# First k of block 0 loaded and turned by itself; block 1's first turns split around a gate product

## The chip, the cores and the metric

The kernel runs on one core of a Trainium2 chip. The metric is the device time of one execution in microseconds (us), the lower the better. A profile gives the same execution from inside: PE is the tensor engine (matrix products; PEld its weight loads), DVE the vector engine, ACT the scalar engine, POOL the engine that issues the converting loads, SP a further issuing engine. Every run also carries the mean clock that was granted to PE.

## The reference, cut to what matters

Linear attention with decay, then a gated feed-forward layer over all tokens:

```python
# q, k, v: (4 batches, 8 heads, 768 positions, 64); weights 512 x 1536, 512 x 1536, 1536 x 512
intra = einsum(q_block, k_block) * decay_mask ; intra = intra @ v_block
inter = (q_block * lam_pow) @ kv_state          # state carried from block to block
x = (intra + inter) as 3072 tokens x 512
out = (sigmoid(x @ w_gate) * (x @ w_val)) @ w_out
```

The kernel works on six blocks of 128 positions. Block 0 has no state yet. The feed-forward layer of a block is cut into 12 units of 128 hidden columns: a gate product, a sigmoid on ACT, a value product, and their product on DVE.

## The kernel before

The traces have each engine's instructions in the order of the program text (before, PE: turns of q 0 from 5.79 us, of q 1 from 6.68, of k 0 and 1 from 7.57, scores from 8.65; ACT: copies of k from 8.01). Only parts are shown. "Turning" is a transpose on PE by a product with the identity; the turned q is scaled by DVE, the turned k is copied out of PSUM by ACT.

```python
# loads, all issued by POOL on one software queue, in this order
load(0, "k", 0, 2)            # k of block 0, batches 0 and 1, one load
load(0, "k", 2, 4)
load(0, "q", 2, 3); load(0, "q", 3, 4)      # q of batches 0 and 1 come by other queues
load(0, "v", 0, 1); load(0, "v", 1, 2); load(0, "v", 2, 3)
load_w(WG, wg_r, 0, GW // 2); load_w(WV, wv_r, 0, GW // 2)   # unit 0
load(0, "v", 3, 4)
load_w(WG, wg_r, 1, GW // 2); load_w(WV, wv_r, 1, GW // 2)   # unit 1: loads 11 and 12
load_w(WG, wg_r, 2, GW // 2)                                 # unit 2, gate: load 13
# ... more weights

def idle(n):                  # dummy products of zeros
    for i in range(n):
        nc.tensor.matmul(wm, lhsT=zero[:, :C], rhs=zero, ...)     # 512 columns

# the start, PE's order
idle(10)
piece_tq0([0]); make_mask(0); idle(1); piece_tq0([1])
piece_tk0(0)                  # turns and copies of k, batches 0 and 1
make_mask(1); idle(1)
piece_s(0, [0]); piece_m(0, 0)              # scores (PE), mask product (DVE)
piece_s(0, [1]); piece_m(0, 1, (0,))
piece_tk0(1)                  # batches 2 and 3
nc.scalar.preload_act_table_set("sigmoid_and_others")
piece_tq0([2]); piece_tq0([3])
piece_m(0, 1, (1,))
piece_s(0, [2], ps_ff, "ff"); piece_m(0, 2); piece_s(0, [3]); piece_m(0, 3)
# ... products with v, casts of x on ACT (piece_a0), first gate product g0

# later, block 1 beside unit 9 of block 0
gv(0, 8)
t(1, 0)                       # turn q, scale; turn k, copy
gv(0, 9)                      # gate product, sigmoid, value product, product
sc(1, 0); m(1, 0)             # scores of block 1
```

Of the kernel before, what the change touches and what calls it, by code (L numbers as in the profile page):

```python
# [8 lines left out]
BF16 = mybir.dt.bfloat16  # L9
# [6 lines left out]
def kernel(  # L16
# [11 lines left out]
    nc = tc.nc  # L28

    B, H, S, D = q.shape  # L30
    C = 128
    NSTEP = S // C
    HP = H // 2
# [4 lines left out]
    TCH = B * C  # L38
# [5 lines left out]
    trsb = ctx.enter_context(tc.tile_pool(name="trsb", bufs=3))  # L44
# [6 lines left out]
    ps_at = ctx.enter_context(tc.tile_pool(name="ps_at", bufs=5, space=bass.MemoryType.PSUM))  # L51
# [9 lines left out]
    WG = const.tile([128, NMT, DFF], BF16, tag="WG")  # L61
    WV = const.tile([128, NMT, DFF], BF16, tag="WV")
# [5 lines left out]
    Q, K, V = {}, {}, {}  # L68

    def load(n, what, b0, b1):  # L70
        sl = slice(n * C, (n + 1) * C)
        for c in what:
            lst, src = {"q": (Q, q), "k": (K, k), "v": (V, v)}[c]
            if n > 1 and c != "v":
                lst[n] = qkv.tile([128, 2, B, HP, D], BF16, tag=c + "b", name=c + "b")
                for e in range(2):
                    nc.gpsimd.dma_start(  # L77
                        out=lst[n][:, e].rearrange("p b y d -> p (b y) d"),
                        in_=src[:, e::2, sl, :].rearrange("b y s d -> s (b y) d"))
                continue  # L80
            if n == 1 and c != "v":
                if n not in lst:
                    lst[n] = qkv.tile([128, 2, B * H * D // 2], BF16, tag=c + "b", name=c + "b")
                for e in range(2):
                    nc.gpsimd.dma_start(
                        out=lst[n][:, b0 // 2].rearrange("p (e x d) -> p e x d", e=2, d=D)[:, e],
                        in_=src[b0:b1, e::2, sl, :].rearrange("b y s d -> s (b y) d"))
                continue
            if n not in lst:
                lst[n] = qkv.tile([128, B, H, D], BF16, tag=c + "b", name=c + "b")  # L90
            nc.gpsimd.dma_start(  # L91
                out=lst[n][:, b0:b1],
                in_=src[b0:b1, :, sl, :].rearrange("b h s d -> s (b h) d"))
# [18 lines left out]
    ident = const.tile([128, 128], BF16, tag="ident")  # L112
# [19 lines left out]
    nc.vector.tensor_scalar(out=ident, in0=ip1, scalar1=p1, scalar2=None, op0=ALU.is_equal)  # L132
    nc.vector.tensor_scalar(out=tri, in0=ip1, scalar1=p1, scalar2=None, op0=ALU.is_ge)

    load(0, "k", 0, 2)
    load(0, "k", 2, 4)
    load(0, "q", 2, 3)
    load(0, "q", 3, 4)
# [61 lines left out]
    def masked(out, x, n, u):  # L200
        if n == 0:
            nc.vector.tensor_tensor(out=out, in0=x, in1=mask[:, u::2, :], op=ALU.mult)
            return
        nc.vector.tensor_tensor(  # L204
            out=out.rearrange("p (e x) c -> p e x c", e=2), in0=x.rearrange("p (e x) c -> p e x c", e=2),
            in1=mask.rearrange("p (x u e) c -> p u e x c", u=2, e=2)[:, u], op=ALU.mult)
# [7 lines left out]
    QS, KS, MT, XT, KD = {}, {}, {}, {}, {}  # L214

    QR, HB = {}, {}
# [20 lines left out]
    def transpose_pair(out, x, b, g):  # L237
        nc.tensor.transpose(out, x[:, b, 2 * g:2 * g + 2, :].rearrange("p h d -> p (h d)"), ident)  # L238

    def scale(n, bp, src):  # L240
        QS[n, bp] = trsb.tile([128, 2, 2, 2, C], BF16, tag="QS", name="QS")
        nc.vector.tensor_tensor(out=QS[n, bp].rearrange("p e i x c -> p e i (x c)"),
                                in0=src.rearrange("p e i x c -> p e i (x c)"),
                                in1=lamq_e.unsqueeze(2).to_broadcast([128, 2, 2, 2 * C]), op=ALU.mult)

    def piece_tq0(bs, then=None):
        tq = ps_at.tile([128, 2, 2, 2 * C], BF16, name="tq", tag="ps")
        for b in bs:
            if (0, b // 2) not in QS:
                QS[0, b // 2] = trsb.tile([128, 2, 2, 2, C], BF16, tag="QS", name="QS")  # L250
            for g in range(HP):
                transpose_pair(tq[:, b % 2, g // 2, g % 2 * C:g % 2 * C + C], Q[0], b, g)
        if then:
            then()
        for b in bs:
            nc.vector.tensor_tensor(out=QS[0, b // 2][:, :, b % 2].rearrange("p e x c -> p e (x c)"),
                                    in0=tq[:, b % 2], in1=lamq0_e, op=ALU.mult)

    def piece_tk0(bp):
        KS[0, bp] = trsb.tile([128, 2, 2, 2, C], BF16, tag="KS", name="KS")  # L260
        for i in range(2):
            if i == 0 or bp == 0:
                tk = ps_at.tile([128, 1 + bp, 2, 2 * C], BF16, name="tk", tag="ps")
            x = tk[:, i if bp else 0]
            for g in range(HP):
                transpose_pair(x[:, g // 2, g % 2 * C:g % 2 * C + C], K[0], 2 * bp + i, g)
            nc.scalar.copy(KS[0, bp][:, :, i].rearrange("p e x c -> p e (x c)"), x)  # L267

    def piece_t(n, bp):
        if n > 1 or bp == 1:  # L270
            scale(n, bp, QR[n][:, :, 2 * bp:2 * bp + 2] if n > 1 else HB["q"])
            return
        q1, k1 = (x[1][:, 0].rearrange("p (e b y d) -> p e b y d", e=2, b=2, y=HP) for x in (Q, K))
        tq = ps_at.tile([128, 2, 2, 2, C], BF16, name="tq", tag="ps")
        tk = ps_at.tile([128, 2, 2, 2, C], BF16, name="tk", tag="ps")

        def turn(out, x):
            for e in range(2):
                for i in range(2):
                    for g in range(2):  # L280
                        nc.tensor.transpose(out[:, e, i, g, :],
                                            x[:, e, i, 2 * g:2 * g + 2, :].rearrange("p y d -> p (y d)"), ident)

        turn(tq, q1)
        scale(n, bp, tq)
        turn(tk, k1)
        KS[n, bp] = trsb.tile([128, 2, 2, 2, C], BF16, tag="KS", name="KS")
        nc.scalar.copy(KS[n, bp], tk)

    SP = {}  # L290

    def piece_s(n, bs, pool=ps_at, tag="ps"):

        for b in bs:
            bp, i = b // 2, b % 2
            sp = [pool.tile([128, HP, C], FP32, name=f"sp{u}", tag=tag) for u in range(2)]
            for hp in range(HP):
                for u in range(2):
                    us = slice(u * 64, (u + 1) * 64)
                    nc.tensor.matmul(sp[u][:, hp, :], lhsT=KS[n, bp][us, hp // 2, i, hp % 2, :],  # L300
                                     rhs=QS[n, bp][us, hp // 2, i, hp % 2, :],
                                     start=(hp == 0), stop=(hp == HP - 1), skip_group_check=True)
            SP[n, b] = sp

    def piece_m(n, b, us=(0, 1)):
        if us[0] == 0:
            MT[n, b] = mtp.tile([128, 2, HP, C], BF16, tag="MT", name="MT")
        for u in us:
            masked(MT[n, b][:, u], SP[n, b][u], n, u)
# [121 lines left out]
    def mm_part(ps, W, n, ft, lo, hi):  # L431
        x = XT[n].rearrange("p m b c -> p m (b c)")
        for mt in range(NMT):
            nc.tensor.matmul(ps[:, lo:hi], lhsT=W[:, mt, ft * 128:(ft + 1) * 128], rhs=x[:, mt, lo:hi],  # L434
                             start=(mt == 0), stop=(mt == NMT - 1))

    def psum():
        return ps_ff.tile([128, TCH], FP32, name="gp", tag="ff")

    def sigm(n, ft, gp):  # L440
        HT[n, ft] = htp.tile([128, TCH], BF16, tag="sg", name="sg", bufs=3)
        nc.scalar.activation(HT[n, ft], gp, AF.Sigmoid)

    def prod(n, ft, vp):
        sg = HT[n, ft]
        HT[n, ft] = htp.tile([128, TCH], BF16, tag="ht", name="ht", bufs=2 * NFT)
        nc.vector.tensor_mul(HT[n, ft], sg, vp)
# [55 lines left out]
    idle(1)  # L503
    piece_tq0([1])
    piece_tk0(0)
    make_mask(1)
    idle(1)
    piece_s(0, [0])
    piece_m(0, 0)
    piece_s(0, [1])  # L510
    piece_m(0, 1, (0,))
    piece_tk0(1)
    nc.scalar.preload_act_table_set("sigmoid_and_others")
    piece_tq0([2])
    piece_tq0([3])
    piece_m(0, 1, (1,))
    piece_s(0, [2], ps_ff, "ff")
    piece_m(0, 2)
    piece_s(0, [3])
# [26 lines left out]
    def t(n, bp):  # L546
        piece_t(n, bp)

    def sc(n, bp):
        piece_s(n, [2 * bp, 2 * bp + 1])  # L550
        piece_m(n, 2 * bp)
# [7 lines left out]
    def gv(n, *fts):  # L559
        for ft in fts:  # L560
            piece_gv(n, ft)
# [36 lines left out]
    lamq_end()  # L598
    gv(0, 6, 7)
    gv(0, 8)  # L600
    t(1, 0)
    gv(0, 9)
    sc(1, 0)
    m(1, 0)
    gv(0, 10)
# [101 lines left out]
```

## Time and profile before

226.63 us, median of three runs (226.24 to 227.24). The profiled run had a span of 224.5 us at full clock.

| reading | value |
|---|---|
| PE busy | 97% of the span |
| chain of waits on PE | 94% |
| first gate product of unit 0 starts | 14.51 us |
| gate, value product of unit 1 start | 17.16, 18.03 us |
| turn of block 1's q, its scores start | 31.45, 34.34 us |

The first part of the page (busy time, share and instructions of each engine):

```profile
PE 217.8 (97%) x1746; PEld 114.7 (51%) x1746; DVE 105.8 (47%) x192; ACT 79.8 (36%) x151; POOL 79.2 (35%) x78
```

So PE is the bound, and time lost on PE after the start is not won back (in the changed kernel it is 1.00 us late at 32.45 us and 1.17 us late at the end, 0.17 of it from unit 9; the table of the result has this). The chain of waits of the kernel before, in order of time (start, duration, what):

```profile
14.09 0.38 ACT XT L352
14.51 1.46 PE gp L434 x8
15.97 0.25 PE op L313 x4
...
16.67 2.39 PE gp L434 x16
19.05 0.37 PE cp L404 x16
...
31.62 0.45 PE tq L281 x8
32.06 0.62 PE tk L281 x8
32.68 0.86 PE gp L420 x4
33.55 0.86 PE vp L426 x4
34.41 0.55 PE sp L300 x16
```

From 16.67 us on every piece is PE's. The first gate product waits for ACT's cast of x. The turn of block 1's k takes 0.62 us and that of q only 0.45: the difference, 0.17 us, is a wait for k's load. The chain times a PE piece by the end of the piece before, so it starts up to 0.2 us later than in the timeline, whose times are used in the text.

### The profile page before, as it was taken

Reading aid. Unit: us, or ns where it says so; the run is one execution under the profiler, and the core shown is the slowest. Engines: PE = TensorE matmul, PEld = TensorE weight load, DVE = VectorE, ACT = ScalarE, POOL = GpSimd, SP = SyncE. Lnnn points to the kernel's source line nnn. Section 1 sums busy time; section 2 is a strip of 40 time slices with the busy share of each in tenths; the row PEclk is TensorE's granted clock in tenths of the full one; section 3 lists DMA queues with packets and bytes.
Section 4 is the critical chain, followed back from the end, with each engine's and each line's share of the span. In section 5 each row is a group of like instructions: output and inputs, shape, how many; then the busy total and the mean of one; then the engine's idle time right before and its main releaser. Section 6 shows DMA issues by size and latency. Waiting matters only on the chain.

```text
span 224.5 us, 4262 instructions
## 1 busy us (share of the span) xinstructions
PE 217.8 (97%) x1746; PEld 114.7 (51%) x1746; DVE 105.8 (47%) x192; ACT 79.8 (36%) x151; POOL 79.2 (35%) x78
## 2 busy tenths in 40 slices
PE   7689999999999999999999999999999999999994
PEld 2454455888854454444445444446444445444443
DVE  7797747595521713336732445742335840333300
ACT  5564334435422234333225333115333225333221
POOL 8996698983592008930006940000000000000000
PEclk9999999999999999999999999999999999999999
DMA  6999999999999992999021999021930012100022
GB/s 109 155 169 193 191 176 155 163 183 168 157 162 159 225 236 86 210 157 101 1 96 55 231 151 128 0 96 47 168 70 0 0 52 91 47 3 0 0 93 95
DMA packets 106419, 25.70 MB, mean 114 GB/s; under 512 B 97056, under 2 KB 103456, under 8 KB 106400
## 3 DMA queue, kind: packets, MB, share of 16 engines
q0 software_dynamic: 81792, 13.90, 81.6%
q1 hardware_dynamic: 23568, 11.28, 20.4%
q10 hardware_dynamic: 1040, 0.26, 0.5%
q8 instruction: 13, 0.21, 0.4%
q14 instruction: 6, 0.05, 0.1%
HBM read 28.32 MB, written 6.29 MB: 154 GB/s over the span
## 4 chain that ended last, share of the span: by engine, by line
PE 94%; DMA 3%; ACT 1%; issue 1%; DVE 0%; POOLq 0%
PE po L483 27%; PE gp L420 21%; PE vp L426 21%; PE gp L455 5%; PE gp L434 5%; PE vp L461 5%; PE sp L300 3%; PE op L313 3%; DMA kb<-in_k_dram 3%; PE op L325 1%; PE po L472 1%; PE cp L404 1%; ACT KS L267 1%; PE tk L238 1%; ACT XT L352 0%
## 5 line engine op out<-in xcount | busy, mean ns | idle before, releaser
L429 DVE TENSOR_TENSOR ht<-sg,vp 128x512 bf16<-128x512 bf16 x54 | 37.1, 687 | 64.2 <-PE vp L426 64.0
L483 PE MATMUL po<-WO,ht 128*128 128x512 bf16 x276 | 62.0, 379 | 0.0
L420 PE MATMUL gp<-XT,WG 128*128 128x512 bf16 x216 | 55.5, 379 | 0.0
L426 PE MATMUL vp<-XT,WV 128*128 128x512 bf16 x216 | 55.4, 379 | 0.0
L423 ACT ACTIVATE sg<-gp 128x512 bf16<-128x512 f32 x54 | 32.2, 597 | 59.0 <-PE gp L420 59.0
L483 PEld LDWEIGHTS <-ht 128*128 128x128 bf16 x276 | 26.3, 98 | 31.0
L426 PEld LDWEIGHTS <-WV 128*128 128x128 bf16 x216 | 21.2, 98 | 25.5
L420 PEld LDWEIGHTS <-WG 128*128 128x128 bf16 x216 | 20.8, 98 | 24.7
L486 ACT COPY ob<-po 128x512 f32<-128x512 f32 x23 | 13.5, 586 | 52.2 <-PE po L483 50.4
L204 DVE TENSOR_TENSOR MT<-sp,mask 128x512 bf16<-128x512 f32 x40 | 25.1, 682 | 9.1 <-PE sp L300 9.1
L382 POOL TENSOR_TENSOR sd<-Sb,dec 128x512 f32<-128x512 bf16 x8 | 8.1, 1037 | 41.2 <-DVE Sb L411 41.1
L455 PE MATMUL gp<-XT,WG 128*128 128x256 bf16 x96 | 14.4, 273 | 0.0
L461 PE MATMUL vp<-XT,WV 128*128 128x256 bf16 x96 | 14.4, 273 | 0.0
L465 DVE TENSOR_TENSOR ht<-sg,vp 128x256 bf16<-128x256 bf16 x24 | 10.0, 420 | 8.6 <-PE vp L461 8.6
L458 ACT ACTIVATE sg<-gp 128x256 bf16<-128x256 f32 x24 | 9.2, 384 | 13.0 <-PE gp L455 11.8
L91 POOL DMA_DIRECT2D vb<-in_v_dram x10 | 12.7, 1278 | 1.0 <-DMA WG<-in_moe_w_gate_dram 0.6
L373 POOL TENSOR_TENSOR kd<-kb,kds 128x1024 bf16<-128x1024 bf16 x6 | 11.3, 1904 | 4.7 <-PE vp L461 4.7
L411 DVE TENSOR_TENSOR Sb<-cp,sd 128x512 bf16<-128x512 f32 x8 | 5.2, 686 | 15.5 <-PE cp L404 15.5
L340 ACT CAST XT<-op 128x512 bf16<-128x512 f32 x19 | 9.9, 598 | 2.1 <-PE op L313 2.0
L455 PEld LDWEIGHTS <-WG 128*128 128x128 bf16 x96 | 9.2, 98 | 1.7 <-issue 0.2
L461 PEld LDWEIGHTS <-WV 128*128 128x128 bf16 x96 | 9.4, 98 | 1.1
L77 POOL DMA_DIRECT2D qb<-in_q_dram x8 | 9.4, 1182 | 0.0
(79 smaller groups left out, 162.1 us busy)
## 6 DMA issues: line engine op xcount, KB each, us to landing
out_dram<-ob SPq DMA_DIRECT2D x21, 256.0 KB, 2.0
kb<-in_k_dram POOLq DMA_DIRECT2D x10, 256.0 KB, 8.4
qb<-in_q_dram POOLq DMA_DIRECT2D x8, 256.0 KB, 8.1
vb<-in_v_dram POOLq DMA_DIRECT2D x4, 512.0 KB, 13.7
WO<-in_moe_w_out_dram POOLq DMA_DIRECT2D x3, 512.0 KB, 8.7
WV<-in_moe_w_val_dram POOLq DMA_DIRECT2D x5, 256.0 KB, 8.8
WG<-in_moe_w_gate_dram POOLq DMA_DIRECT2D x4, 256.0 KB, 8.6
qb<-in_q_dram POOLq DMA_DIRECT2D x6, 128.0 KB, 8.3
```

What stands on the lines that cost most here:

```text
L91: nc.gpsimd.dma_start(out=lst[n][:, b0:b1], in_=src[b0:b1, :, sl, :].rearrange("b h s d -> s (b h) d"))
L204: nc.vector.tensor_tensor(out=out.rearrange("p (e x) c -> p e x c", e=2), in0=x.rearrange("p (e x) c -> p e x c", e=2), in1=mask.rearrange ...
L373: nc.gpsimd.tensor_tensor(out=KD[n][:, e], in0=K[n][:, e], in1=kds[:, e::2].unsqueeze(1).unsqueeze(3).to_broadcast([128, B, HP, D]), op=AL ...
L420: nc.tensor.matmul(gp, lhsT=WG[:, mt, fs], rhs=x[:, mt, :], start=(mt == 0), stop=(mt == NMT - 1))
L423: nc.scalar.activation(sg, gp, AF.Sigmoid)
L426: nc.tensor.matmul(vp, lhsT=WV[:, mt, fs], rhs=x[:, mt, :], start=(mt == 0), stop=(mt == NMT - 1))
L429: nc.vector.tensor_mul(HT[n, ft], sg, vp)
L434: nc.tensor.matmul(ps[:, lo:hi], lhsT=W[:, mt, ft * 128:(ft + 1) * 128], rhs=x[:, mt, lo:hi], start=(mt == 0), stop=(mt == NMT - 1))
L455: nc.tensor.matmul(gp[:, cs], lhsT=WG[:, mt, fs], rhs=x[:, mt, cs], start=(mt == 0), stop=(mt == NMT - 1))
L461: nc.tensor.matmul(vp[:, cs], lhsT=WV[:, mt, fs], rhs=x[:, mt, cs], start=(mt == 0), stop=(mt == NMT - 1))
L483: nc.tensor.matmul(po, lhsT=HT[n, ft][:, tt * 128:(tt + 1) * 128], rhs=WO[:, ft, :], start=(ft == 0), stop=(ft == NFT - 1))
L486: nc.scalar.copy(ob, po)
```

## The change

Its intent: the first scores should not wait for the k of batch 1, and the wait for block 1's k load should vanish under a gate product.

```diff
-    load(0, "k", 0, 2)
+    load(0, "k", 0, 1)
+    load(0, "k", 1, 2)
     load(0, "k", 2, 4)
...
     idle(1)                      # piece_tk0 now takes batches; piece_tk0(0) before it turns batch 0 alone
     piece_s(0, [0])
     piece_m(0, 0)
+    piece_tk0(1)
     piece_s(0, [1])
-    piece_m(0, 1, (0,))
-    piece_tk0(1)
+    piece_m(0, 1)
+    piece_tk0(2, 3)
     nc.scalar.preload_act_table_set("sigmoid_and_others")
     piece_tq0([2])
     piece_tq0([3])
-    piece_m(0, 1, (1,))
...
     gv(0, 8)
-    t(1, 0)
-    gv(0, 9)
+    scale(1, 0, turn(Q))
+    g9 = psum()
+    mm_part(g9, WG, 0, 9, 0, TCH)
+    sigm(0, 9, g9)
+    tk = turn(K)
+    KS[1, 0] = trsb.tile([128, 2, 2, 2, C], BF16, tag="KS", name="KS")
+    nc.scalar.copy(KS[1, 0], tk)
+    v9 = psum()
+    mm_part(v9, WV, 0, 9, 0, TCH)
+    prod(0, 9, v9)
     sc(1, 0)
```

The extra load moves every later load of POOL's queue one place back: the value weights of unit 1 become load 13.

More of the change, by code (lines that the diff above doesn't have):

```diff
@@ L257, in piece_tq0, with piece_tk0 @@
                                     in0=tq[:, b % 2], in1=lamq0_e, op=ALU.mult)
-    def piece_tk0(bp):
-        KS[0, bp] = trsb.tile([128, 2, 2, 2, C], BF16, tag="KS", name="KS")
-        for i in range(2):
-            if i == 0 or bp == 0:
-                tk = ps_at.tile([128, 1 + bp, 2, 2 * C], BF16, name="tk", tag="ps")
-            x = tk[:, i if bp else 0]
+    def piece_tk0(*bs):
+        bp = bs[0] // 2
+        if (0, bp) not in KS:
+            KS[0, bp] = trsb.tile([128, 2, 2, 2, C], BF16, tag="KS", name="KS")
+        tk = ps_at.tile([128, len(bs), 2, 2 * C], BF16, name="tk", tag="ps")
+        for j, b in enumerate(bs):
@@ L265, in piece_tk0 @@
             for g in range(HP):
-                transpose_pair(x[:, g // 2, g % 2 * C:g % 2 * C + C], K[0], 2 * bp + i, g)
-            nc.scalar.copy(KS[0, bp][:, :, i].rearrange("p e x c -> p e (x c)"), x)
+                transpose_pair(tk[:, j, g // 2, g % 2 * C:g % 2 * C + C], K[0], b, g)
+            nc.scalar.copy(KS[0, bp][:, :, b % 2].rearrange("p e x c -> p e (x c)"), tk[:, j])
     def piece_t(n, bp):
-        if n > 1 or bp == 1:
-            scale(n, bp, QR[n][:, :, 2 * bp:2 * bp + 2] if n > 1 else HB["q"])
-            return
@@ L273, in piece_t @@
-        q1, k1 = (x[1][:, 0].rearrange("p (e b y d) -> p e b y d", e=2, b=2, y=HP) for x in (Q, K))
-        tq = ps_at.tile([128, 2, 2, 2, C], BF16, name="tq", tag="ps")
-        tk = ps_at.tile([128, 2, 2, 2, C], BF16, name="tk", tag="ps")
-        def turn(out, x):
-            for e in range(2):
-                for i in range(2):
-                    for g in range(2):
-                        nc.tensor.transpose(out[:, e, i, g, :],
-                                            x[:, e, i, 2 * g:2 * g + 2, :].rearrange("p y d -> p (y d)"), ident)
@@ L284, in piece_t, with turn @@
-        turn(tq, q1)
-        scale(n, bp, tq)
-        turn(tk, k1)
-        KS[n, bp] = trsb.tile([128, 2, 2, 2, C], BF16, tag="KS", name="KS")
-        nc.scalar.copy(KS[n, bp], tk)
+        scale(n, bp, QR[n][:, :, 2 * bp:2 * bp + 2] if n > 1 else HB["q"])
+    def turn(x):
+        x = x[1][:, 0].rearrange("p (e b y d) -> p e b y d", e=2, b=2, y=HP)
+        out = ps_at.tile([128, 2, 2, 2, C], BF16, name="tq", tag="ps")
+        for e in range(2):
+            for i in range(2):
+                for g in range(2):
+                    nc.tensor.transpose(out[:, e, i, g, :],
+                                        x[:, e, i, 2 * g:2 * g + 2, :].rearrange("p y d -> p (y d)"), ident)
+        return out
```

## The prediction

> **What bounds it now.** The tensor engine: the page has PE busy 97% of a 224.5 us span; the chain of waits is 94% PE and 3% the first k load, at a granted clock of 1.0. From about 16 us on PE streams almost without idle time, so what PE loses there is lost for good, and little can be won outside the first 16 us.
>
> **Start (0 to 16 us).** The chain of waits runs: first k (two batches) issued 1.26, landed 7.53; its eight turns from 7.57; two ACT copies 8.01 to 9.08; scores from 8.65; DVE's mask products from 9.08. [...] One-batch loads follow each other at about 0.85 us, so I estimate batch 0 landed at 6.5 to 6.8. The turns of q batch 1, ahead in PE's order, wait for ACT's cast (ends 6.63); so the turns of k run about 6.95 to 7.35, one copy ends at 7.9, scores of batch 0 start near 8.0 (0.65 us earlier), and DVE starts its mask products at about 8.4, where the second mask ends anyway.
>
> I don't think this reaches the end. (1) The scores of batch 1 now follow their own turn and copy (scores 9.5 to 9.9), and the turns of k 2, 3 and q 2, 3 follow them, so the scaling of q 2 moves from 11.18 to about 11.6. DVE holds the same work (eight mask products of 0.62, two scalings of 0.38) with two new holes, and ends within 0.2 us of before (14.9). (2) PE then waits for loads: v of batch 2 at 13.51, the first WG at 14.23, WV at 15.0, v of batch 3 at 15.90, all from one continuous stream of descriptors. [...] the DMA view shows them saturated from about 4 us by both q loads, so an earlier k takes its share from q batch 1 and the stream behind does not move, or moves 0.1 us later by the extra load. Worth: -0.1 us (-0.35 to +0.15).
>
> **Unit 9.** Before: turns of q 31.45, turns of k with a 0.17 us wait for k's load (at 32.28), gate, value, scores at 34.34; ACT's copy of k (1.01 us, 32.72 to 33.73) hid under gate and value. After: the load wait vanishes under the gate product. But the gate ends at about 32.95, its sigmoid holds ACT to 33.57, and the copy of k, queued behind it, runs 33.57 to 34.58. The value product ends at 34.24. So the scores start at about 34.62, not 34.34: PE waits about 0.45 us and wins 0.17. Worth: +0.28 us, kept to the end.
>
> **Sum.** 226.63 - 0.1 + 0.28 = 226.8 us, range 226.2 to 227.5. Chances: faster by over 2% 0.005, within 2% 0.99, slower by over 2% 0.005.
>
> **What would show it.** Timeline: scores of batch 0 near 8.0; scores of batches 2, 3 near 12 (11.66 before); gate product of unit 0 within 0.3 us of 14.51; v of batch 3 still waited for near 15.9. Unit 9: scores from 34.5 or later, a new PE wait for ACT of 0.3 to 0.5 us; no wait for k's load.
>
> **What would make it wrong.** The load stream starting 0.3 us earlier[...]: v and WG land earlier and the start wins up to 0.4 us. The value product hiding more of the copy than I reckon. Or q batch 1 landing so late that the early scores gain nothing.

Passages that told of the hardware without a trace of this case are cut from the recorded texts, here and below, and the cuts are marked. No term of the sum is among them: it came to 226.63 - 0.1 + 0.28 = 226.8 us and still does. The -0.1 has lost a part of its argument, that on how loads of several queues share the DMA engines. What the trace of the kernel before shows is: the core's DMA engines ("them" in the text) at 90% or more from 3.6 us on (the DMA view of 0 to 8 us), and loads 3 to 7 of POOL's queue landing 0.83 to 0.87 us apart. From the latter comes the estimate for batch 0's k: 7.53 - 0.85 = 6.7 us.

## More of the kernel before

ACT's timeline of the kernel before at the start (start, duration, engine and line, operation, what, count, and in brackets the idle time before and who ended it):

```profile
9.90 0.59 ACT L267 COPY KS<-tk 128x512 bf16<-128x512 bf16 x1 [0.82 <-PE tk L238]
10.96 0.59 ACT L267 COPY KS<-tk 128x512 bf16<-128x512 bf16 x1 [0.47 <-PE tk L238]
11.56 1.28 ACT L513 ACT_TABLE_LOAD   x1
12.85 1.07 ACT L352 CAST XT<-op 128x512 bf16<-128x512 f32 x2
14.09 0.65 ACT L352 CAST XT<-op 128x256 bf16<-128x256 f32 x2 [0.16 <-PE op L313]
```

Between the last copy of k and the first cast of x stands the load of the sigmoid table, 1.28 us, with no idle time on either side.

## The result, and the profile after

227.77 us, median of six runs (227.13 to 228.14), against 226.65 (226.24 to 227.24, six runs). The ratio is 1.0042, 95% interval 1.0021 to 1.0064. Ratios here and below are the mean time of one kernel's fast runs over that of the other's of the same rounds, so not quite the ratio of the medians. The time lies outside the predicted range, on the slow side.

The profiled run has a span of 225.6 us, also at full clock, 1.17 us over the one before (225.65 and 224.48 unrounded). The same instructions, placed in both timelines:

| instruction starts | before | after | later by |
|---|---|---|---|
| scores of batch 0 | 8.65 | 8.30 | -0.35 |
| scaling of q, batch 2 | 11.18 | 11.75 | 0.57 |
| gate product, unit 0 | 14.51 | 14.82 | 0.31 |
| gate product, unit 1 | 17.16 | 17.48 | 0.32 |
| value product, unit 1 | 18.03 | 19.01 | 0.98 |
| turn of block 1's q | 31.45 | 32.45 | 1.00 |
| scores of block 1 | 34.34 | 35.51 | 1.17 |
| end | 224.48 | 225.65 | 1.17 |

Three steps make the loss in this execution: 0.31 us at the start, 0.66 us between the gate and the value product of unit 1, 0.17 us at unit 9 (and 0.03 of rounding and drift). The chain of waits after:

```profile
11.84 7.13 DMA WV<-in_moe_w_val_dram
18.96 0.05 issue
19.01 1.04 PE gp L427 x4
20.05 0.37 PE cp L397 x16
...
32.61 0.45 PE tq L279 x8
33.06 0.88 PE gp L427 x4
33.93 0.02 issue
33.96 0.47 ACT sg L435
34.42 0.03 issue
34.45 1.01 ACT KS L600
35.47 0.05 issue
35.51 0.62 PE sp L293 x16
```

A load of weights is now on the chain, 7.13 us from issue to landing, where the four loads ahead of it took 5.5 to 5.6, and PE waits for it. At unit 9, ACT's sigmoid and its copy of k have come into the chain between PE's pieces; k's load has left it.

ACT's timeline after, the lines that answer to those of before:

```profile
10.47 0.59 ACT L268 COPY KS<-tk 128x512 bf16<-128x512 bf16 x1 [0.82 <-PE tk L239]
11.53 0.59 ACT L268 COPY KS<-tk 128x512 bf16<-128x512 bf16 x1 [0.47 <-PE tk L239]
12.13 1.28 ACT L507 ACT_TABLE_LOAD   x1
13.42 1.63 ACT L345 CAST XT<-op 128x512 bf16<-128x512 f32 x4
```

The copies of k 2 and 3 come 0.57 us later, the table load and the first cast with them. 0.26 us of the 0.57 is absorbed, 0.31 us reaches the first gate product.

PE itself is why the copies are late. The waits of PE (who waited for whom, us in total, times, longest), before, those for copies of k alone:

```profile
PE tk L238 <- ACT KS L267: 0.7, 1, 0.7
PE sp L300 <- ACT KS L267: 0.2, 1, 0.2
```

and after:

```profile
PE sp L293 <- ACT KS L268: 1.1, 2, 0.7
PE tk L239 <- ACT KS L268: 0.7, 1, 0.7
PE gp L427 <- DMA WV<-in_moe_w_val_dram: 0.5, 1, 0.5
PE sp L293 <- ACT KS L600: 0.3, 1, 0.3
```

The scores of batch 1 stand behind their own turn and copy: 0.68 us of PE doing nothing at 9.7 us, with the turns of batches 2 and 3 queued behind. PE's busy time in the stretch from 7.8 to 11.2 us, by the view of windows (us of the stretch, then busy us of PE, PEld, DVE, ACT, POOL; granted clock; DMA), first before:

```profile
7.80:11.20 3.40, 2.40 (x40) 1.66 (x37) 2.46 (x5) 1.90 (x4) 3.40 (x6) 1.00 2.43 155
```

and after:

```profile
7.80:11.20 3.40, 1.59 (x27) 1.05 (x27) 3.01 (x6) 1.62 (x3) 3.40 (x6) 1.00 2.43 155
```

PE is busy 1.59 us instead of 2.40.

**One late DMA engine.** Why did PE wait for a load that was nearly all there in time? The trace has sixteen completions of each load, and the page counts 16 DMA engines for the core. The completions of two loads, in order of time (us, after):

```
load 12, gate weights of unit 1:  15.34 15.43 15.94 ... 16.53 16.55 16.55 16.57
load 13, value weights of unit 1: 16.07 16.14 16.69 ... 17.33 17.33 17.35 18.96
```

Fifteen completions of load 13 are there at 17.35; PE goes on at 19.01, 0.05 us after the sixteenth (18.96). I read each completion as that of one DMA engine; the packet records name no engine, so this is not shown. "A late engine" is in this document a last completion far behind the others, "the fifteenth engine" the one before it in time. Here it is 1.6 us behind, and about 1.1 us in the loads that followed (load 14: 18.07 and 19.18; load 16: 20.12 and 21.19). The packet records show one foreign packet at that time: 16,384 bytes on the instruction queue, starting at 16.92 us and taking 0.95 us. That leaves the rest of the 1.6 us unexplained by the records. The page counts these packets:

```profile
q8 instruction: 13, 0.21, 0.4%
```

The line is the same before and after: 13 packets, 0.21 MB. In the trace of before they stand on average 124 weight loads and 124 products of PE apart (138 weight loads ahead of the first packet, 1625 ahead of the thirteenth; 84 to 179 from one to the next). That they bring PE's instructions is an inference, from the name of the queue and from `before_30`, below: with 30 more pairs of weight load and product in front, the first packet comes at 15.06 us instead of 16.84, again behind 138 weight loads. This is what "fetch" means from here on. In the kernel before, the packet at 16.84 us goes with a late engine as well (18.98 against 17.97 for the fifteenth), but there the load in flight is number 13, the gate weights of unit 2, not needed until 19.36.

### The profile page after: what moved, and what is told of

It reads as the page before. It is cut to its first block, busy times and chain, and to the rows that moved or that the text cites. A ratio compares the mean times of both kernels' runs of the same rounds, so it can differ in the third digit from the quotient of the medians.

```text
span 225.6 us, 4240 instructions
## 1 busy us (share of the span) xinstructions
PE 215.7 (96%) x1723; PEld 114.4 (51%) x1746; DVE 105.3 (47%) x192; ACT 79.8 (35%) x151; POOL 79.9 (35%) x79
## 4 chain that ended last, share of the span: by engine, by line
PE 89%; POOL 5%; DMA 3%; issue 1%; ACT 1%; DVE 0%; POOLq 0%
PE po L476 27%; PE gp L413 21%; PE vp L419 20%; PE gp L448 5%; PE vp L454 5%; PE gp L427 4%; DMA WV<-in_moe_w_val_dram 3%; PE sp L293 2%; PE op L306 2%; POOL vb L91 2%; PE op L318 1%; POOL kb L91 1%; PE po L465 1%; PE cp L397 1%; POOL qb L91 1%
## 5 line engine op out<-in xcount | busy, mean ns | idle before, releaser
L422 DVE TENSOR_TENSOR ht<-sg,vp 128x512 bf16<-128x512 bf16 x53 | 36.5, 688 | 62.6 <-PE vp L419 58.3
L476 PE MATMUL po<-WO,ht 128*128 128x512 bf16 x266 | 61.3, 379 | 0.5
L413 PE MATMUL gp<-XT,WG 128*128 128x512 bf16 x207 | 54.0, 379 | 0.4
L419 PE MATMUL vp<-XT,WV 128*128 128x512 bf16 x208 | 53.5, 379 | 0.1
L416 ACT ACTIVATE sg<-gp 128x512 bf16<-128x512 f32 x53 | 31.6, 597 | 58.9 <-PE gp L413 57.8
```

The lines of the kernel that those rows point to most:

```text
L413: nc.tensor.matmul(gp, lhsT=WG[:, mt, fs], rhs=x[:, mt, :], start=(mt == 0), stop=(mt == NMT - 1))
L416: nc.scalar.activation(sg, gp, AF.Sigmoid)
L419: nc.tensor.matmul(vp, lhsT=WV[:, mt, fs], rhs=x[:, mt, :], start=(mt == 0), stop=(mt == NMT - 1))
L422: nc.vector.tensor_mul(HT[n, ft], sg, vp)
L476: nc.tensor.matmul(po, lhsT=HT[n, ft][:, tt * 128:(tt + 1) * 128], rhs=WO[:, ft, :], start=(ft == 0), stop=(ft == NFT - 1))
```

## The experiments

Theory A, formed from the two traces: (1) the new order delays ACT's copies, table load and casts, 0.3 us; (2) the extra load puts the value weights of unit 1 in flight when an instruction fetch holds up one DMA engine, 0.66 us, by chance from run to run; (3) unit 9 waits for ACT's copy, 0.17 us. Theory E came with the first runs: (4) in the new order PE idles enough for its clock to be halved for a while in some runs. Rivals: B, unit 9 is the whole loss (the prediction's account); C, the extra load just pushes the stream; D, the 13th load is late whatever happens (its place in the queue).

All kernels gave correct results. The runs of the kernel before, in the four calls with rounds, had medians of 226.63, 226.56, 226.94 and 226.67 us.

### 1 to 4: the parts alone

`p1_start` is the changed kernel with unit 9 put back:

```diff
     scale(1, 0, turn(Q))
-    g9 = psum(); mm_part(g9, WG, 0, 9, 0, TCH); sigm(0, 9, g9)
     tk = turn(K)
     KS[1, 0] = trsb.tile(...); nc.scalar.copy(KS[1, 0], tk)
-    v9 = psum(); mm_part(v9, WV, 0, 9, 0, TCH); prod(0, 9, v9)
+    gv(0, 9)
```

> Only the start of the change (own load of batch 0's k, its turn ahead of the first scores), unit 9 as before. Theory A, read from the two traces: the start costs 0.3 us (the turns and copies of k 2 and 3, and with them the table load and the casts on ACT, come 0.57 us later, and the first gate product starts at about 14.8 instead of 14.5), and the value product of unit 1 waits for its weights, about 0.65 us, because a 16 KB instruction fetch at about 16.9 us holds up one DMA engine while just that load is in flight. So ratio 1.003 to 1.005, about +0.9 us. Rival B, the prediction's own account: the start is neutral and unit 9 makes the loss: ratio 0.999 to 1.001.

`p2_unit9` is the kernel before with only the unit 9 part of the change.

> Only unit 9's part of the change, start as before. Theory A: scores of unit 9 start 3.06 us after the turn of q instead of 2.89, with a PE wait of about 0.3 us for ACT's copy of k and none for k's load: +0.17 us, ratio 1.0005 to 1.0012. Rival B: this part is the whole loss: +0.9 us, ratio about 1.004. The start must read as in the kernel before (first gate product at 14.5, no wait for the value weights of unit 1).

`load_only` is the kernel before with only the k load split:

```diff
-    load(0, "k", 0, 2)
+    load(0, "k", 0, 1)
+    load(0, "k", 1, 2)
```

> The kernel before with nothing but the k load of batches 0 and 1 split in two; turns and scores in the old order. Theory A: the copies on ACT stay where they were (first gate product at 14.5 to 14.6), but the value weights of unit 1 become the 13th load of the queue instead of the 12th and are in flight at 16.9 us when the instruction fetch comes; if it hits an engine that still holds part of them the value product of unit 1 waits 0.3 to 1.0 us, and the ratio is 1.001 to 1.004; the landing of that load is then over 6.5 us after its issue, and the other 15 engines' parts land by 17.4. Rival C, that the extra load only pushes the stream by its own cost: each landing 0.1 us later, no wait over 0.2 us, ratio 1.000 to 1.001.

`order_only` is `p1_start` with one k load:

```diff
-    load(0, "k", 0, 1)
-    load(0, "k", 1, 2)
+    load(0, "k", 0, 2)
```

> The new order of turns and scores at the start, but k of batches 0 and 1 in one load as before; unit 9 as before. Theory A: the turns wait for the whole load (7.5), all of the ACT chain comes 0.3 us later than in the changed kernel, the first gate product at about 15.0, so +0.5 us, and no wait for the value weights of unit 1, since the gate weights of unit 2 are in flight at the fetch again: ratio 1.0015 to 1.003. Rival B: within 0.1 us of before. Rival C (the order is harmless, the load does it): ratio 1.000.

Measured (six runs each):

| kernel | ratio, 95% interval | gate product, unit 0 | PE waits for value weights, unit 1 |
|---|---|---|---|
| p1_start | 1.0053, 1.0034 to 1.0072 | 14.86 | 0.47 |
| p2_unit9 | 1.0017, 0.9997 to 1.0036 | 14.43 | no |
| load_only | 1.0020, 1.0001 to 1.0038 | 14.55 | 0.72 |
| order_only | 1.0038, 1.0012 to 1.0064 | 14.96 | no |

B falls: the start alone has the whole loss (1.0053 against the change's 1.0042; the intervals overlap). C falls: with nothing changed but the split of a load, the chain of `load_only` shows PE held for a load that took 7.06 us:

```profile
11.91 7.06 DMA WV<-in_moe_w_val_dram
18.98 0.05 issue
19.02 1.04 PE gp L435 x4
```

Its first gate product starts at 14.55, as before (14.51), so the split does not make the late start; `order_only`, with 14.96, shows that the order does. In `order_only` the late engine is again at load 13, the gate weights of unit 2, and PE does not wait. Its ratio is above the 1.0015 to 1.003 that were expected: three of its six runs have a lowered clock, which had not been reckoned with (the list of runs below). `p2_unit9` has the wait for the copy, in the view of waits:

```profile
PE sp L292 <- ACT KS L599: 0.3, 1, 0.3
```

Its scores start 3.07 us after the turn of q (34.45 and 31.38), against 2.89 before: 0.18 us, as expected; its interval includes 1.

The spread of the runs told something that no profile had shown. Each run with its granted clock, where it was under 0.998:

```
after       227.13 227.20 227.76 227.78 | 228.01 (0.992) 228.14 (0.992)
p1_start    227.42 | 227.81 227.92 227.95 227.97 (all 0.992) 228.71 (0.985)
order_only  226.87 226.88 227.43 | 227.77 227.95 (0.992) 228.79 (0.985)
load_only   226.55 226.91 227.42 227.43 227.45 227.48
p2_unit9    226.69 226.71 226.74 227.24 227.51 227.51
```

The three kernels with the new order have a lower clock in 10 of 18 runs; `load_only` and `p2_unit9` in none of 12, the kernel before in none of the 44 runs of the calls with rounds. One profile fell in a run with a lower clock, that of `fill`, below: mean 0.992, and in its clock record one stretch of 3.41 us at half the clock. By an estimate from that trace, one such stretch in its span of 225.1 us is a mean of 1 - 0.5 x 3.41 / 225.1 = 0.992, and two are 0.985, the two values that the runs show; no run at 0.985 was profiled. And among runs at full clock there are two groups, 0.5 to 0.9 us apart; `load_only` has four runs in the upper one, among them the profiled one (227.42), which has the wait.

### 5 to 8: moving the fetch, filling the waits

`before_fewer` and `load_fewer` were to move the instruction fetch later, by fewer instructions in the warm-up, on the kernel before and on `load_only`:

```diff
-    idle(10)                 # bf16, 512 columns
+    idle_wide(5)             # fp32, 256 columns, the same zeros
```

> The kernel before, with its ten 128x512 bf16 warm-up products replaced by five 128x256 fp32 products of zeros that should hold PE as long: about 15 to 19 fewer PE instructions ahead of everything[...]. Theory A: the first instruction fetch moves from 16.8 to 17.2 us or later, when the value weights of unit 1 have landed on all engines; then no run is held up there: the runs gather in the lower of the two groups seen before (226.3 to 226.7, none near 227.2), ratio 0.998 to 0.9995. Rival D, that the late engine belongs to the 13th load of the queue[...] whatever the fetch does: the fetch moves or not, the late engine stays at the 13th load, ratio 1.000 with the same two groups.

> The split k load alone (as in load_only), with the same fewer-instructions warm-up. Theory A: the fetch comes after the value weights of unit 1 have landed, so the wait at about 18 to 19 us of load_only goes, ratio 0.998 to 1.000 against before, about 0.7 us under load_only's upper group (227.4). Rival D: the 13th load, which is here the value weights of unit 1, stays late and PE waits 0.5 to 0.7 us: ratio 1.002 as load_only.

`before_more` has more instructions in its warm-up:

```diff
-    idle(10)
+    idle(6)
+    idle_narrow(16)          # 32 columns
```

> The kernel before, with four of its ten warm-up products replaced by sixteen of 32 columns: 24 more PE instructions ahead of everything[...]. Theory A: the fetch comes 0.5 to 1.5 us earlier (15.4 to 16.3 us) and the engine it hits is late by 0.7 to 1.6 us from the 11th or 12th load on (gate or value weights of unit 1), so PE waits 0.4 to 1.0 us for one of them around 17 to 18.5 us: ratio 1.002 to 1.004, nearly all runs above 227.0. Rival D[...]: the late engine stays at the 13th load, no wait, ratio 1.000.

`p1_warm` is `p1_start` with dummy products in PE's new waits:

```diff
     piece_tk0(1)
+    idle(2)
     piece_s(0, [1])
     piece_m(0, 1)
-    piece_tk0(2, 3)
+    piece_tk0(2, 3, between=lambda: idle(2))
     ...
     piece_tq0([3])
+    idle(1)
```

> The start of the change alone (p1_start), with dummy products of 512 columns in its new PE waits: two before the scores of batch 1, two between the turns of k 2 and 3, one after the turns of q. Theory E: the new order leaves PE busy only 1.6 us of the 3.4 us from 7.8 to 11.2, against 2.4 before, so that in some runs the clock is halved[...] (granted clock 0.992 or 0.985 in 10 of 18 runs of the kernels with the new order, in none of 23 with the old): with the waits filled, all runs show a clock of 0.999 or 1.0, the runs at 227.8 and above go, and the median falls from 227.9 to about 227.3 (ratio 1.002 to 1.004), the late start and the wait for the value weights of unit 1 staying. Rival: the low clocks came by chance or from something else on the chip: they stay in about half of the runs, ratio 1.005.

The two "fewer" kernels failed as manipulations: in the trace the five fp32 products are ten, with ten weight loads (4.63 us of PE, where the ten of the kernel before took 4.45), so no instruction was saved and the fetch did not move (16.79 and 16.96 us). What they measured is a repetition: `before_fewer` 1.0003 (0.9987 to 1.0018), `load_fewer` 1.0025 (1.0010 to 1.0041), with the wait (0.68 us) again in the profile of the split load (the value weights land at 18.98, PE goes on at 19.03; the view names an ACT instruction that ended at the same time). The expected gain was not tested.

`before_more` moved the fetch to 16.42 us, and the late engine moved from load 13 to load 12, the value weights of unit 1 (17.01 on the fifteenth engine, 18.50 on the last). Its ratio is 1.0024 (1.0011 to 1.0036), all six runs at 226.96 or above. But its PE also came later to that load (first gate product at 14.91: its clock record is full only from 10.05 us on, in the kernel before from 6.03, and the eight turns of k took 1.03 us instead of 0.62; that the narrow products did this is not shown), and waited under 0.15 us for it. So it shows where the late engine goes, not what that costs.

`p1_warm` has a clock of 0.998 or more in all six runs, against one of six in `p1_start`; 227.20 us, ratio 1.0027 (1.0013 to 1.0041), against 1.0053. So in these runs the lowered clock goes with PE's waits in the new order. The ratios would make it about half of what `p1_start` lost, but that share is an estimate: in the profiled run of `p1_warm` the fetch had moved as well. The late start stayed (14.98). The expectation that the wait for the value weights would stay too was not met in the profiled run: its fetch came at 16.26, and no load up to 13 was late.

Why only some runs are hit is not shown. An estimate from the traces, over stretches as long as the slow one of `fill` (3.41 us): the least that PE is busy in any such stretch that starts between 4 and 16 us is 1.96 us in the kernel before, 1.60 in `p1_start`, `order_only` and the change (starting near 7.8), and 1.83 in `p1_warm`. But `before_30`, below, has a stretch with 1.67 and a full clock in all five runs, so no rule comes out of these numbers.

### 9 to 12: a clean move of the fetch, and attempts to mend

`before_30` cuts the warm-up into products of 128 columns, 30 more pairs of weight load and product with as many columns in all:

```diff
-    idle(10)                 # 512 columns
+    idle_short(40)           # 128 columns
```

> The kernel before, its ten 512-column warm-up products cut into forty of 128 columns: same time for PE, 60 more PE instructions. (The five fp32 products tried first were ten in the trace, so the fetch had not moved.) Theory A: the first instruction fetch moves well ahead, to 13.5 to 15.5 us, and one engine is late by 0.7 to 1.6 us from the 8th to 11th load on (v of batch 3, or gate or value weights of units 0 and 1) instead of the 13th; PE then waits for that load 0.5 to 1.0 us between 14 and 18.5 us in most runs: ratio 1.003 to 1.005, lowest run above 226.8. Rival D (the 13th load is late whatever the fetch does): ratio 1.000, the late engine at the 13th load.

The fetch moved to 15.06 us, the late engine to load 10, the v of batch 3 (15.59 on the fifteenth engine, 17.12 on the last), and PE waited 1.40 us for it (0.5 to 1.0 were expected). The first gate product was on time, 14.30. Its chain:

```profile
9.57 7.55 DMA vb<-in_v_dram
17.12 0.04 issue
17.16 0.32 PE op L318 x4
```

1.0035 (1.0023 to 1.0047), all five fast runs between 227.66 and 227.75. Nothing of the work was changed here, only the number of PE's instructions ahead of it: 138 weight loads stand ahead of the first packet, just as in the kernel before. Part 2 of theory A holds, and D falls: the late engine follows the fetch, not the place in the queue.

`load_merged` is `load_only` with the q loads of batches 2 and 3 made one, `best_start` is `p1_start` with that and with k 2 turned before the scores of batch 1:

```diff
+    load(0, "q", 2, 4)          # both kernels, for the two loads
-    load(0, "q", 2, 3)
-    load(0, "q", 3, 4)
     # best_start only
     piece_tk0(1)
+    piece_tk0(2)
     piece_s(0, [1])
-    piece_m(0, 1)
-    piece_tk0(2, 3)
+    piece_m(0, 1, (0,))
+    piece_tk0(3)
     nc.scalar.preload_act_table_set("sigmoid_and_others")
     piece_tq0([2])
     piece_tq0([3])
+    piece_m(0, 1, (1,))
```

> The split k load alone, but with the two q loads of batches 2 and 3 made one, so that the value weights of unit 1 are again the 12th load and land again by about 17.2 us. Theory A: the wait at 18 to 19 us becomes as rare as before (a third of the runs or fewer): ratio 0.999 to 1.001, against 1.002 of the split alone; in the profile the late engine is that of the 13th load, the gate weights of unit 2. If the wait stays in most runs at a 12th load that lands on time on 15 engines, the count of loads is not what matters, and the ratio stays at 1.002.

> An attempt to have the early scores without their price: the start of the change with k of batch 2 turned before the scores of batch 1 (so that PE doesn't stand still for the copy of k 1), each turn in its own PSUM tile, DVE in the old order, q of batches 2 and 3 in one load; unit 9 as before. Theory A: the first gate product starts at 14.2 to 14.5 (14.8 in the changed kernel), no run has a clock under 0.998, the late engine is at the 13th load again; the load of v of batch 3 (15.8) limits the gain to about 0.1 us: ratio 0.9985 to 1.0005. If the order of turns isn't what costs at the start, the gate product stays at 14.8 and the ratio at 1.0015 or more.

`load_merged`: 1.0008 (0.9994 to 1.0023), four of six runs at 226.76 to 226.89, the late engine at load 13, no wait. But the first gate product came at 14.96, since the merged q lands later (the turns of q start at 11.19 instead of 10.76). One of its runs had a clock of 0.992, in the old order.

`best_start` missed: 1.0025 (1.0013 to 1.0037), gate product at 14.80. The merge was my mistake, PE waited 0.54 us for q at 11.03. And the value weights of unit 1, now load 12, were hit all the same, by a fetch at 16.93 (17.31 and 18.98). So being load 12 is no protection, which is a second count against D.

`u9_halves` is `p2_unit9` with k copied in two halves, ahead of the sigmoid:

```diff
-    sigm(0, 9, g9)
-    tk = turn(K)
+    tk = turn(K, by="i")        # batch by batch
     KS[1, 0] = trsb.tile(...)
-    nc.scalar.copy(KS[1, 0], tk)
+    for i in range(2):
+        nc.scalar.copy(KS[1, 0][:, :, i], tk[:, :, i])
+    sigm(0, 9, g9)
```

> The kernel before with unit 9's part alone, but ACT copies the turned k in two halves (by batch), ahead of the sigmoid of unit 9, so that the scores of the first batch wait for half a copy. Theory A: after the turn of k the scores need only about 0.6 us of copy instead of 1.0, which the value product (0.86 us) covers: scores start at most 2.8 us after the turn of q (2.89 before, 3.06 in the change), no PE wait over 0.15 us for the copy: ratio 0.999 to 1.0005, against 1.0017 with the copy in one. If the scores still start 3.0 us or more after the turn of q, the copy was not what they waited for.

The timeline of `u9_halves`:

```profile
33.27 1.07 ACT L600 COPY KS<-tq 128x512 bf16<-128x512 bf16 x2 [2.02 <-PE tq L279]
34.03 0.77 PE L293 MATMUL sp<-QS,KS 64*128 64x128 bf16 x16
```

The scores start while the second half is copied, 2.72 us after the turn of q (31.31), without a wait of PE. 226.46 us median, ratio 0.9990 (0.9976 to 1.0005). This is the intent of the change at unit 9, met; it is the fastest kernel of the study by its median, and its interval does not meet that of the change as made (1.0021 to 1.0064, from another call). Against the kernel before the interval includes 1, so a gain is not shown.

### 13 and 14: the late start by itself

`fill` is `p1_start` with the order of `best_start` and the loads of the change.

> The start of the change alone (p1_start), with k of batch 2 turned before the scores of batch 1, each turn of k in its own PSUM tile, and DVE's old order (scaling of q 2 and 3 ahead of the last mask product of batch 1); loads as in the change. If the late start comes from PE standing still for the copy of k 1, with the turns of k 2, 3 and q 2, 3 and so the copies, the table load and the casts of ACT behind it: the scaling of q 2 starts at 11.2 or earlier (11.75 in the change), the first cast at 12.9 or earlier (13.42) and the first gate product at 14.3 to 14.6 (14.8). If it comes from something else, such as the later landing of the loads, the gate product stays at 14.8. The value weights of unit 1 are the 13th load, so PE still waits for them in most runs: ratio 1.001 to 1.003; no clock under 0.998.

It ran at 1.0013 (0.9997 to 1.0030), but its profile fell in an execution with a halved clock. Its granted clock, and then PE's timeline in the slow stretch:

```profile
core 0: 225.1 us, clock 0.992
```

```profile
8.49 0.57 PE L293 MATMUL sp<-QS,KS 64*128 64x128 bf16 x8 [0.46 <-ACT KS L268]
8.99 1.15 PE L239 MATMUL tk<-ident,kb 128*128 128x128 bf16 x8
```

The clock record of this trace has 0.5 from 8.57 to 11.98 us, for 3.41 us. Eight turns take 1.15 us in it, where they took 0.62 in the kernel before. In a stretch as long just ahead of it (5.15 to 8.57) PE was busy 1.84 us. The slow stretch starts before the wait at 9.7, which is what `fill` fills, so with that wait filled a slow stretch can still come (one of six runs here). Nor does the busy time ahead of it settle the matter: in the trace of `load_merged` PE was busy 1.79 us in a stretch as long (4.10 to 7.51), and the clock stayed full.

The same kernel:

> As for fill, at full clock: scaling of q 2 at 11.2 or earlier, first cast at 12.9 or earlier, first gate product at 14.3 to 14.6. If the late start has another cause than the order of the turns: gate product at 14.8. If the clock is halved again, nothing can be read.

At full clock, ACT's timeline reads:

```profile
9.90 1.24 ACT L268 COPY KS<-tk 128x512 bf16<-128x512 bf16 x2 [0.17 <-PE tk L239]
11.16 1.28 ACT L508 ACT_TABLE_LOAD   x1
12.84 1.07 ACT L345 CAST XT<-op 128x512 bf16<-128x512 f32 x2 [0.40 <-PE op L306]
```

The table load starts at 11.16 (12.13 in the change), the first cast at 12.84 (13.42), the first gate product at 14.58 (14.82). With the turn of k 2 moved into PE's wait, the table load and the casts come early again. In this one execution that takes back 0.24 of the 0.31 us, so the late start is the order of the turns and what stood behind them. The three edits of `fill` (the moved turn, the PSUM tiles of their own, DVE's old order) were not tried one by one. The span was 224.5 us, that of before; its fetch came at 16.17 and held up nothing that was waited for.

### What the fetch met in each trace

```
kernel         fetch at  first load with a late engine      15th engine  last   PE waits
before_30        15.06   10, v of batch 3                      15.59     17.12   1.40
fill_again       16.17   none up to load 13                                      no
p1_warm          16.26   none up to load 13                                      no
before_more      16.42   12, value weights of unit 1           17.01     18.50   under 0.15
p2_unit9         16.47   13, gate weights of unit 2            17.88     18.58   no
before_fewer     16.79   13, gate weights of unit 2            17.82     18.95   no
u9_halves        16.82   13, gate weights of unit 2            17.83     18.95   no
before           16.84   13, gate weights of unit 2            17.97     18.98   no
after            16.92   13, value weights of unit 1           17.35     18.96   0.50
p1_start         16.93   13, value weights of unit 1           17.38     18.97   0.47
load_only        16.93   13, value weights of unit 1           17.46     18.98   0.72
best_start       16.93   12, value weights of unit 1           17.31     18.98   0.55
order_only       16.94   13, gate weights of unit 2            17.81     19.01   no
load_fewer       16.96   13, value weights of unit 1           17.50     18.98   0.68
load_merged      17.10   13, gate weights of unit 2            18.25     19.21   no
```

`fill` (17.11) is left out, its clock was halved. In all thirteen rows with a late engine its completion comes 2.02 to 2.16 us after the start of the fetch, from 15.06 to 17.10 us: the strongest sign that the fetch is the cause. The time of the fetch is not fixed by the program alone: in `fill_again` 117 weight loads stood ahead of it, in `fill`, the same kernel, 134. Open: which engine the fetch takes, and so why it is harmless in one execution and not in another (`fill_again`, `p1_warm`), the records do not tell. They do show a difference: the packet took 0.89 us in `fill`, `fill_again`, `p1_warm`, `p2_unit9` and `load_merged`, where the last engine is at most 0.96 us behind the fifteenth in the loads up to 13, and 0.94 to 0.97 us in the other eleven, where it is 1.0 to 1.7 us behind. That would fit another engine; it is not shown. Nor were the upper groups of runs of the kernel before (up to 227.24) profiled.

## Why the prediction was wrong, point by point

- **The bound, and that PE's losses stay:** right. The 1.00 us that PE was late at the turn of block 1's q was still there at the end.
- **The early scores don't reach the end:** right in kind. The scores of batch 0 came 0.35 us earlier, not 0.65, because q of batch 1 landed at 6.31 instead of 5.99 us, while k of batch 0 landed at 6.75 instead of 7.53: the earlier k came with a later q, as predicted, but by more. The scaling of q 2 moved to 11.75 (predicted 11.6).
- **"Worth: -0.1 us (-0.35 to +0.15)" for the start:** this term was wrong; the start cost 0.31 us in the profile. The step that failed was to follow DVE and the loads and not ACT. From the last copy of k on, the copy, the table load and the casts form one chain without idle time, and it was pushed by 0.57 us. `order_only` has the delay with the old loads, `fill_again` takes most of it away with the new ones.
- **"The stream behind does not move, or moves 0.1 us later by the extra load":** right for v of batch 3 (landed at 15.85 instead of 15.75) and for fifteen of the sixteen completions of the value weights of unit 1 (by 17.35), and yet wrong where it counted. The prediction treated a load as landed when the stream has passed. It overlooked that one completion can fall behind (18.96), and that the extra load changes which load is exposed. That term, 0.66 us in the profiled run, was missing from the sum altogether; `load_only` has it alone, `before_30` makes it by moving the fetch.
- **The lowered clock:** also missing. The prediction saw "two new holes" on DVE and did not ask what PE's own holes do to its clock. `p1_warm` against `p1_start` shows it in these runs: 0 of 6 runs with a clock under 0.998 against 5 of 6 (the ratios, 1.0027 against 1.0053, hold the moved fetch as well).
- **Unit 9, "+0.28 us":** sign and mechanism right, size 0.17. The load wait went, and PE waited 0.28 us for the copy. The part given to the sigmoid was small: the copy started 0.08 us after the turn's end (34.37 by the timeline). The cause is that the copy (1.01 us, from the end of the turn) takes longer than the value product (0.86 us by the chain) that was to cover it; half a copy is short enough (`u9_halves`).

The sum for a run at full clock: 226.6 + 0.31 + 0.17 = 227.1 us without the wait for the weights, and 227.7 with it. The six runs are 227.13 and 227.20, 227.76 and 227.78, and two of 228.0 and 228.1 at the lower clock. That the first pair had no wait is an inference from the sum; only the run of 227.76 was profiled, and it had one.

## What to carry to other kernels

When one step is moved forward in an in-order program, look at what now stands behind its wait on every engine: here the first scores won 0.35 us and the work of three other batches paid for it. Where a stream of loads is only just in time, ask for the last of the sixteen completions of a load and for anything else that moves at that time: here one load more, or 30 more pairs of PE instructions, changed which load had the late one, and PE waited 0.50 us (the change) and 1.40 us (`before_30`). And read the run list with its clocks before reading a profile: the profile shows one execution, and here the largest differences between runs were not in it (`p1_start`: profiled at 227.42 us, its slowest run 228.71 at a clock of 0.985).
